# A fused causal convolution and spectral mixing kernel: other banks for the last mixings, another split of evictions in the second unit, and another route for the last bank

## The chip, the cores and the metric

The kernel runs on one core of a Trainium2 chip. The metric is the device time of one execution in microseconds. Three runs of the kernel before took 173.77, 173.94 and 174.34 us; the median, 173.94 us, is what the forecast is measured against. Beside these there is one profiled execution, of which the page and the trace tell.

## The reference

The input is x with 8 sequences of 3264 positions and 192 channels, in float32. Two stages follow each other.

The first is a causal convolution along the sequence. Each of 8 heads (24 channels each) has 7 taps, made by a softmax over its 7 weights:

```
w = softmax(weight, axis=-1)
out[b, s, h*24:(h+1)*24] = sum_k w[h, k] * x[b, s - 6 + k, h*24:(h+1)*24]
```

The second takes this output as its own x, and mixes it in frequency:

```
X  = rfft(x, axis=1)
Yr = einsum('bmd,mde->bme', Xr, w_r) - einsum('bmd,mde->bme', Xi, w_i)   # modes 0..63 only
Yi = einsum('bmd,mde->bme', Xr, w_i) + einsum('bmd,mde->bme', Xi, w_r)
y  = irfft(Y, n=3264, axis=1)                                            # all other modes are 0
u  = x + y
out = u + maximum(u @ w_ch, 0)
```

So each position gets u = x + y, and to it relu(u W) with a 192 by 192 matrix W.

## The kernel before, in words

Everything is in bf16 except the sums in PSUM and the output. The work is issued in the order in which it is written: the code runs under a manual schedule, so each engine's queue holds its instructions in program order, and semaphores for the data and for the buffers are added to it.

**Tiles.** The 8 sequences are taken as 4 pairs. A sequence is cut into blocks of 256 positions, 13 of them (the last has 192), and a block into its even and odd positions, which makes 26 tiles of 128 positions for a pair, 104 in all. `xall` holds x, and later the convolved x in its place. The last block's tiles use 96 partitions.

**Convolution (L288 to L345).** The pairs are cut into units, two for each pair; I number them 1 to 8. Units 1 and 2 belong to the first pair and have 5 and 8 blocks (`UNITS0`); the others have 7 and 6. For each unit the loop runs over the 8 heads, numbered 0 to 7, and for each head over the even and the odd positions. A head takes 16 small matmuls (L297), and its upper half lags two steps behind its lower half. For the first pair, a head's two results go to a tile of two PSUM banks, and there are four such tiles; one instruction then evicts both into `xall`, cast to bf16, on ScalarE (L334) or on VectorE (L336). Line 333 chooses between them. A tile goes back to the free list once it is evicted, and head h+4 takes the tile of head h. The tables of sine and cosine for the Fourier products are made in between (L192 to L210): VectorE works out the angles, ScalarE the sine. x comes in by DMA, issued by POOL (L153, L157), a unit at a time and in the order of the units; the weights of the mixing follow in the same queue (L276). Unit 1's convolution is followed by the first six Fourier products and three matmuls that write nothing that is used (L434).

**Fourier sums and mixing.** Products with the table `ftab` (L358) give the 64 modes, which are transposed (L375, L377) into `xt`. There are 16 mixings, numbered 0 to 15, of four modes each. A mixing (L510, L515) is 12 matmuls into the half of a bank; two mixings share one bank. ScalarE scales the result into `ymix` (L527), TensorE transposes it into two banks (L546 by way of L398), and VectorE (L552) and ScalarE (L554) copy the two into `yet`. Meanwhile the convolved x is transposed into `ct`.

**The products with W (L587 to L604).** For each pair of sequences, numbered 0 to 3, `zw_pair` multiplies `yet` by two halves of the weights: eight matmuls (L591, L592) into two banks, of which ScalarE evicts the first (L602) and VectorE the second (L604) into `zwl`. Pairs 1, 2 and 3 are done early, with the last eight modes still zero or incomplete in `yet`; `late_rows` works out those rows apart and sends them over the rows in `zwl` by 16 small DMAs. Pair 0 is done last, when `yet` is complete (L681 to L687).

**Banks of the mixing tail.** There are eight banks: `ze` (two) and `zm` (two) on the right side, and `sl` (four) on the left side, opened at L664. Before the change `place[0]` and `place[1]`, the banks of the first two row-tile pairs of the second stage, are all four of `sl`; `zw_pair(1)` and `zw_pair(3)` use `ze`, `zw_pair(2)` uses `zm`; mixing 14 goes to `zm[1]`, mixing 15 to `zm[0]`; and both transposes of a mixing go to `ze`.

**Second stage (L695 to L767).** It runs over 52 duos of an even and an odd tile, 104 items in all. For each item, matmuls (L711) compute u W into a bank, ScalarE applies the relu in place (L637), a matmul adds y to the same bank, and VectorE adds x and writes float32 to an output buffer (L624). The banks are handed out from a list of eight, `ring`, in turn. An item is worked on by halves of the array, so TensorE has several items open. The last two items take y in one full matmul each (`full`, L644). Once both items of a duo are added, SP issues one store (L632) of 384 KB, or 288 KB for the last duo of each pair of sequences. For the first and the last duo of all, each item is stored apart; the last duo's items are 144 KB each.

Of the kernel before, what the change touches and what calls it, by code (L numbers as in the profile page):

```python
# [9 lines left out]
ALU = mybir.AluOpType  # L10
# [10 lines left out]
def kernel(  # L21
# [9 lines left out]
    nc = tc.nc  # L31
    B, S, D = x.shape
# [8 lines left out]
    NT = 2 * NB  # L41
# [13 lines left out]
    def sb(name, shape, dtype):  # L55
        return pool.tile([P] + shape, dtype, tag=name, name=name)
# [6 lines left out]
    xall = sb("xall", [NSLOT, 2, D], BF16)  # L63
# [13 lines left out]
    ident = sb("ident", [P], BF16)  # L77
    perm = sb("perm", [P], BF16)
    apart = [sb(f"apart{i}", [P], BF16) for i in range(2)]
# [112 lines left out]
    def table(step, t0, t1):  # L192
# [15 lines left out]
        else:  # L208
# [5 lines left out]
                            in1=wmax.unsqueeze(2).to_broadcast([P, H, KK]), op=ALU.subtract)  # L214
# [11 lines left out]
    for h0 in (0, H // 2):  # L226
        hs = slice(h0, h0 + H // 2)
        for lag in range(KK):
            k = lag // 2
            nc.vector.copy_predicated(  # L230
                out=pk4[:, hs, lag % 2, :],
                mask=masks[:, PW * k:PW * (k + 1)].unsqueeze(1).to_broadcast([P, H // 2, PW]),
                data=ta3[:, hs, KK - 1 - lag:KK - lag].to_broadcast([P, H // 2, PW]))
        for g in range(4):
            c0 = 1 + 32 * (g % 2)
            dst, srcv = band[32 * g:32 * g + 32, hs, :, c0:c0 + PW], pk4[32 * g:32 * g + 32, hs, :, :]
# [34 lines left out]
    NG = MODES // 4  # L271

    def load_w(g):
        if g < NG:
            for half, src in ((0, moe_w_r), (1, moe_w_i)):
                nc.gpsimd.dma_start(out=wts[g][64 * half:64 * half + 64, :, :, :],  # L276
                                    in_=src[4 * g:4 * g + 4, :, :].rearrange("m (p j) e -> p m j e", j=3))

    def turn(names):
        nop = nc.tensor.nop()  # L280
        for name in names:
            tc.add_manual_dep(nop.ins, name, mybir.DependencyInfo(mybir.DependencyClass.Sync,
                                                                  mybir.DependencyReason.DATA),
                              reason="row tiles take turns on a bank")

    def conv_pieces(step, row):

        (q, b0, n, h, a), z, _ = step  # L288
        s0 = NB * q + b0 + 1
        r = slice(64 * row, 64 * row + 64)  # L290
        dsl = slice(GRP * h, GRP * h + GRP)
        for a1 in range(2):
            for col in (row, 1 - row):
                c0 = (0 if a < a1 else 1) + (64 if col != row else 0)
                s1 = s0 - 1 if (row, col) == (1, 0) else s0
                o = z[64 * col:64 * col + 64, 0:2 * GRP * n].rearrange("p (b i e) -> p b i e", b=n, i=2)
                yield nc.tensor.matmul(o, band[r, h, int(a != a1), c0:c0 + 64], xin5[r, s1:s1 + n, :, a1, dsl],  # L297
                                       start=(row == 0 and a1 == 0), stop=(row == 1 and a1 == 1),
                                       tile_position=(64 * row, 64 * col), skip_group_check=True).ins.name
# [4 lines left out]
    def conv_step(u):  # L304

        lower = upper = iter(())
        flow.append(None)
        if u is not None:
            if u[0]:
                z = free.pop(0)  # L310
            else:
                z = flow[-2][0][2] if u[4] else free.pop(0)
            flow[-1] = [(u, z[:, u[4] if u[0] == 0 else 0, :], z), []]
            lower = conv_pieces(flow[-1][0], 0)
        old = flow[-1 - CONVLAG] if len(flow) > CONVLAG else None
        if old is not None:
            upper = conv_pieces(old[0], 1)

        if u is not None:
            flow[-1][1].extend(lower)  # L320
        if old is not None:
            turn(old[1][2:])
            for _ in upper:
                pass
        if old is None or old[0][0][4] == 0:
            return
        (q, b0, n, h, _), _, tile1 = old[0]
        s0 = NT * q + 2 * b0
        dst = xall[:, s0:s0 + 2 * n, :, GRP * h:GRP * h + GRP].rearrange("p (b a) i e -> p a b i e", a=2)
        tile0 = flow[-2 - CONVLAG][0][2]  # L330
        if q == 0:
            srcv = tile0[:, :, 0:2 * GRP * n].rearrange("p a (b i e) -> p a b i e", b=n, i=2)
            if h not in (5, 7) if b0 == 0 else h % 2 == 0:
                nc.scalar.copy(out=dst, in_=srcv)  # L334
            else:
                nc.vector.tensor_copy(out=dst, in_=srcv)  # L336
            free.append(tile0)
        else:
            for a, z in enumerate((tile0, tile1)):
                srcv = z[:, 0, 0:2 * GRP * n].rearrange("p (b i e) -> p b i e", b=n, i=2)  # L340
                if a == 1:
                    nc.scalar.copy(out=dst[:, a], in_=srcv)  # L342
                else:
                    nc.vector.tensor_copy(out=dst[:, a], in_=srcv)  # L344
                free.append(z)  # L345

    def flush():
        for _ in range(CONVLAG):
            conv_step(None)
        flow.clear()  # L350
# [125 lines left out]
    ze, zm = [z[:, 0, :] for z in z4[0:2]], [z[:, 0, :] for z in z4[2:4]]  # L476
# [33 lines left out]
    def mix(g, bank):  # L510
        yp = bank[:, D * (g % 2):D * (g % 2) + D]
        for j in range(3):
            for p4 in range(4):
                m = 4 * g + p4
                nc.tensor.matmul(yp[32 * p4:32 * p4 + 2 * B, :], xt[:, j, :, m],  # L515
                                 wts[g][:, p4, j, :], start=(j == 0), stop=(j == 2),
                                 tile_position=(0, 32 * p4), skip_group_check=True)
        load_w(g + NW + NL)

    def mix_copy(d, bank, g0, n):  # L520

        g = 2 * d + g0
        srcv = bank[:, D * g0:D * (g0 + n)].rearrange("p (g d) -> p g d", g=n)
        if g == 0:
            nc.scalar.activation(out=ymix[:, 0, :], in_=srcv[:, 0, :], func=ACT.Copy, scale=ascale[:, 0:1])
            g, n, srcv = 1, n - 1, srcv[:, 1:n, :]
        nc.scalar.activation(out=ymix[:, g:g + n, :], in_=srcv, func=ACT.Copy, scale=2.0 / S)  # L527
# [66 lines left out]
    def zw_pair(q, bw, by):  # L594

        for t, bank in enumerate((bw, by)):
            for i in range(2):
                zw_mm(2 * q + i, bank[:, D * i:D * i + D], t)
        for t, bank in enumerate((bw, by)):
            dst, srcv = zwl[:, 2 * q - 2:2 * q, t, :], bank[:, 0:2 * D].rearrange("p (b d) -> p b d", b=2)  # L600
            if t == 0:
                nc.scalar.copy(out=dst, in_=srcv)  # L602
            else:
                nc.vector.tensor_copy(out=dst, in_=srcv)  # L604
# [9 lines left out]
    duos = [((q, 2 * b), (q, 2 * b + 1)) for q in range(NQ) for b in range(NB)]  # L614
    N = len(duos)
    place = {}

    def add(bank, n, a):

        o = outs[n % NO]  # L620
        q, t = duos[n][0]
        pn = PL if t == NT - 2 else P
        s = NT * q + t
        nc.vector.tensor_tensor(out=o[0:pn, :, a, :],  # L624
                                in0=bank[0:pn, 0:2 * D].rearrange("p (i d) -> p i d", i=2),
                                in1=xall[0:pn, s + a, :, :], op=ALU.add)
        apart = n in (0, N - 1)
        if apart or a == 1:
            a0, w = (a, 1) if apart else (0, 2)
            dst = bass.AP(tensor=out.tensor, offset=out.offset + (2 * q * S + P * t + a0) * D,  # L630
                          ap=[[2 * D, pn], [S * D, 2], [1, w * D]])
            nc.sync.dma_start(out=dst, in_=o[0:pn, :, a0:a0 + w, :].rearrange("p i a d -> p i (a d)"))  # L632
# [8 lines left out]
    def full(n, which, a):  # L641
        (q, t), _ = duos[n]
        r = zrhs(slice(0, P), which, q)
        nc.tensor.matmul(target(place[n][a], slice(0, 2 * D), r), ftab[:, t + a, :], r, start=False,  # L644
                         stop=(which == "y"), skip_group_check=True)
# [13 lines left out]
    d = ND - 2  # L659
# [2 lines left out]
    mix(2 * d + 1, zm[0])  # L662
    mix_copy(d, zm[0], 0, 2)
    sl = [z[:, 0, :] for z in open_psum("left", (1, 1, 1, 1))]  # L664
    place[0], place[1] = sl[0:2], sl[2:4]
    both(0, 0, "c", begin=True)
    mix_trans(d, 0, 2)
    both(0, 1, "c")
    zw_pair(1, ze[0], ze[1])
    zw_pair(2, zm[0], zm[1])  # L670
    d = ND - 1
    mix(NG - 2, zm[1])
    mix_copy(d, zm[1], 0, 1)
    zw_pair(3, ze[0], ze[1])
    mix_trans(d, 0, 1)
    mix(NG - 1, zm[0])
    mix_copy(d, zm[0], 1, 1)
    both(1, 0, "c", begin=True)
    mix_trans(d, 1, 1)
    both(1, 1, "c")  # L680
# [15 lines left out]
    LAG = 2  # L696
    items = [(n, a) for n in range(FIRST, N) for a in range(2)]
    K = len(items)
    ring = ze + zm[1:2] + sl + zm[0:1]
    taken = [0]  # L700

    def next_of_ring():
# [3 lines left out]
    bank = {}  # L706
# [23 lines left out]
    def lower_y(k):  # L730
        if 0 <= k < K - 2:
            product(k, 0, pieces(k, 0, "y")[0], False, False)
        elif K - 2 <= k < K:
            n, a = items[k]
            full(n, "y", a)
            add(bank[k], n, a)

# [62 lines left out]
```

## Time and profile before

| what | value |
|---|---|
| median of three runs | 173.94 us (173.77 to 174.34) |
| profiled execution | 173.73 us, of which the span is 171.9 us |
| TensorE matmuls | 161.4 us busy, 94% of the span |
| VectorE | 129.6 us busy, 75% |
| ScalarE | 113.1 us busy, 66% |
| the chain that ended last | TensorE 83%, VectorE 8%, ScalarE 3% |
| granted TensorE clock, mean | 0.997 |
| DMA | 39.10 MB read, 20.05 MB written |

The page's times are in microseconds from the first instruction. A line of the timeline or of the chain begins with its start and its length; then come the engine, the tile and the line of the kernel, and "x12" for a group of twelve instructions. In square brackets stands how long the engine was idle before it, and who released it. A matmul's row is longer than the distance to the next matmul, since they are pipelined. The span by stages, from the chain: convolution and Fourier sums up to some 72 us, mixing and transposes up to 105 us, second stage from 106 to 167 us, and the last stores.

### The profile page before, as it was taken

What the parts mean: (1) busy time and instruction counts of PE and PEld (TensorE: products, weight loads), DVE (VectorE), ACT (ScalarE), POOL (GpSimd) and SP (SyncE); (2) the same over time, 40 slices, a digit from 0 to 9 for tenths busy, and PEclk for the clock granted to TensorE, in tenths of its full rate; (3) what the DMA queues carried; (4) which work ended last, traced back from release to release, by engine and by line L of the source; (5) the groups of instructions that cost most, each with busy time, mean ns of one, the idle gap of its engine ahead of it and who ended that gap; (6) DMA issues with size and microseconds to landing.
All of it is one profiled execution on the core that took longest, in us unless ns stands there. A gap on an engine that the chain in (4) does not pass through costs nothing.

```text
span 171.9 us, 6922 instructions
## 1 busy us (share of the span) xinstructions
PE 161.4 (94%) x2896; PEld 134.8 (78%) x2896; DVE 129.6 (75%) x263; ACT 113.1 (66%) x225; POOL 51.4 (30%) x93
## 2 busy tenths in 40 slices
PE   6998899999998999979999979999999999999990
PEld 6994686877867777779999765699999999999960
DVE  4899974736737575567767734799999999999991
ACT  8485864545546366377777643688888888888870
POOL 7997522323322443444431000691000000000000
PEclk9999999999999999999999999999999999999998
DMA  3999999999999999999999940389989999899996
GB/s 28 201 203 203 207 201 203 204 203 202 205 202 205 208 205 206 207 206 206 209 204 207 209 79 4 105 305 328 372 322 338 348 330 343 317 366 341 338 349 219
DMA packets 37359, 40.14 MB, mean 233 GB/s; under 512 B 2480, under 2 KB 37328, under 8 KB 37328
## 3 DMA queue, kind: packets, MB, share of 16 engines
q0 software_dynamic: 22816, 19.62, 71.3%
q1 hardware_dynamic: 14512, 20.09, 31.9%
q8 instruction: 22, 0.36, 0.8%
q14 instruction: 9, 0.07, 0.1%
HBM read 39.10 MB, written 20.05 MB: 344 GB/s over the span
## 4 chain that ended last, share of the span: by engine, by line
PE 83%; DVE 8%; ACT 3%; issue 2%; POOL 1%; DVEq 0%; POOLq 0%; ACTq 0%
PE z L711 34%; PE z L297 19%; PE z L398 12%; PE z L358 10%; PE z L515 3%; DVE arena L230 2%; DVE xall L336 1%; POOL xall L153 1%; PE z L591 1%; PE z L644 1%; DVE shared L240 1%; PE z L375 1%; PE z L592 1%; DVE arena L604 1%; DVE arena L624 1%
## 5 line engine op out<-in xcount | busy, mean ns | idle before, releaser
L624 DVE TENSOR_TENSOR arena<-z,xall 128x384 f32<-128x384 f32 (+1 forms) x104 | 57.4, 557 | 2.9 <-PE z L711 0.8
L637 ACT ACTIVATE z<-z 128x384 f32<-128x384 f32 x102 | 48.5, 475 | 12.2 <-PE z L711 2.4
L711 PEld LDWEIGHTS <-ct 64*128 64x128 bf16 x600 | 42.4, 94 | 3.7 <-PE z L644 0.6
L711 PE MATMUL z<-arena,ftab 64*128 64x384 bf16 x308 | 44.9, 322 | 0.0
L297 PE MATMUL z<-xall,shared 64*64 64x336 bf16 (+3 forms) x1024 | 38.5, 294 | 1.2 <-DVE xall L336 0.7
L297 PEld LDWEIGHTS <-shared 64*64 64x64 bf16 x1024 | 33.2, 106 | 6.6 <-issue 4.4
L711 PE MATMUL z<-wsw,ct 64*128 64x192 bf16 x300 | 35.1, 243 | 0.0
L711 PEld LDWEIGHTS <-ftab 64*128 64x128 bf16 x396 | 29.7, 93 | 2.7 <-issue 0.5
L344 DVE CAST xall<-z 128x336 bf16<-128x336 f32 (+1 forms) x48 | 22.9, 483 | 11.5 <-PE z L297 9.0
L711 PE MATMUL z<-wm,ct 64*128 64x192 bf16 x200 | 29.9, 243 | 0.0
L342 ACT CAST xall<-z 128x336 bf16<-128x336 f32 (+1 forms) x48 | 19.9, 419 | 13.8 <-PE z L297 10.0
L711 PE MATMUL z<-w,ct 64*128 64x192 bf16 x100 | 24.3, 243 | 0.0
L395 DVE COPY ct<-z 128x1024 bf16<-128x1024 bf16 x27 | 17.4, 685 | 5.5 <-PE z L398 2.4
L398 PE MATMUL z<-ident,xall 128*128 128x128 bf16 x312 | 19.8, 219 | 0.0
L358 PE MATMUL z<-xall,ftab 128*128 128x384 bf16 (+1 forms) x104 | 18.3, 327 | 0.8 <-DVE xall L336 0.8
L398 PEld LDWEIGHTS <-xall 128*128 128x128 bf16 x312 | 17.8, 98 | 1.0 <-issue 0.2
L153 POOL DMA_DIRECT2D xall<-in_x_dram x16 | 15.0, 942 | 10.4 <-DMA xall<-in_x_dram 9.6
L358 PEld LDWEIGHTS <-ftab 128*128 128x128 bf16 (+1 forms) x104 | 9.6, 98 | 8.2 <-issue 1.5
L711 PE MATMUL z<-mixa,ftab 64*128 64x384 bf16 x88 | 13.6, 323 | 0.0
L393 ACT COPY ct<-z 128x1024 bf16<-128x1024 bf16 x12 | 12.2, 1013 | 2.1 <-PE z L398 1.9
L539 POOL DMA_DIRECT2D arena<-xs x16 | 7.9, 505 | 17.2 <-ACT xs L535 17.2
L184 PE MATMUL z<-xall 128*128 128x144 bf16 x85 | 8.1, 280 | 1.6 <-DVE xall L171 1.6
(110 smaller groups left out, 154.2 us busy)
## 6 DMA issues: line engine op xcount, KB each, us to landing
out_dram<-arena SPq DMA_DIRECT2D x47, 384.0 KB, 3.6
xall<-in_x_dram POOLq DMA_DIRECT2D x8, 672.0 KB, 16.9
xall<-in_x_dram POOLq DMA_DIRECT2D x8, 480.0 KB, 16.7
arena<-in_moe_w_r_dram POOLq DMA_DIRECT2D x10, 288.0 KB, 11.2
arena<-in_moe_w_i_dram POOLq DMA_DIRECT2D x10, 288.0 KB, 11.5
ct<-in_moe_w_r_dram POOLq DMA_DIRECT2D x6, 288.0 KB, 11.5
ct<-in_moe_w_i_dram POOLq DMA_DIRECT2D x6, 288.0 KB, 11.5
out_dram<-arena SPq DMA_DIRECT2D x3, 288.0 KB, 3.2
```

The costliest lines, as they stand in the source:

```text
L153: nc.gpsimd.dma_start(out=xin[:, s0:s0 + nf, 2 * D * i:2 * D * (i + 1)], in_=src)
L184: nc.tensor.matmul(free[3][:, 0, 0:144], zeros[:, 0:P], zeros[:, 0:144], start=True, stop=True, skip_group_check=True)
L297: yield nc.tensor.matmul(o, band[r, h, int(a != a1), c0:c0 + 64], xin5[r, s1:s1 + n, :, a1, dsl], start=(row == 0 and a1 == 0), stop=(row ...
L342: nc.scalar.copy(out=dst[:, a], in_=srcv)
L344: nc.vector.tensor_copy(out=dst[:, a], in_=srcv)
L358: nc.tensor.matmul(xp, ftab[0:k, t, :], xall[0:k, NT * q + t, :, :], start=(t == t0), stop=(t == t1 - 1), skip_group_check=True)
L393: nc.scalar.copy(out=out, in_=in_)
L395: nc.vector.tensor_copy(out=out, in_=in_)
L398: nc.tensor.matmul(o, in_, ident[:], start=True, stop=True, is_transpose=True)
L624: nc.vector.tensor_tensor(out=o[0:pn, :, a, :], in0=bank[0:pn, 0:2 * D].rearrange("p (i d) -> p i d", i=2), in1=xall[0:pn, s + a, :, :], o ...
L637: nc.scalar.activation(out=z, in_=z, func=ACT.Relu)
L711: mm = nc.tensor.matmul(target(bank[k], cols, r), l, r, start=first, stop=last, skip_group_check=True)
```

## The change

The change has three parts.

1. **Evictions in unit 2.** Line 333 gives heads 0, 1, 3 and 5 of unit 2 to ScalarE and heads 2, 4, 6 and 7 to VectorE. Before, ScalarE had the even and VectorE the odd heads. In unit 1 nothing changes (ScalarE has 0, 1, 2, 3, 4 and 6).
2. **Banks of the mixing tail.** Mixings 14 and 15 both go to `zm[1]`. The transposes of mixing 14 stay in `ze`, those of mixing 15 go to the two banks that `ze` is renamed to, `sl[2:4]`; `place[1]` gets the old `ze` in exchange. `zw_pair(2)` moves behind mixing 14 and uses `sl[2]` and `sl[3]`; `zw_pair(3)` moves behind the transposes of mixing 14 and uses `zm[0]` and `sl[2]`. The list `ring` is written so that the new banks take the old roles in it.
3. **The very last bank.** For the last item of all, TensorE multiplies the identity by x into the bank (384 columns), ahead of the product that adds y, and ScalarE copies the bank to the output buffer; VectorE adds nothing there. The last duo is stored by one DMA of 288 KB after both items, where there were two of 144 KB.

```diff
@@ conv_step
-            if h not in (5, 7) if b0 == 0 else h % 2 == 0:
+            if h in ((0, 1, 2, 3, 4, 6) if b0 == 0 else (0, 1, 3, 5)):
                 nc.scalar.copy(out=dst, in_=srcv)
             else:
                 nc.vector.tensor_copy(out=dst, in_=srcv)
@@ add
-        nc.vector.tensor_tensor(out=o[0:pn, :, a, :],
-                                in0=bank[0:pn, 0:2 * D].rearrange("p (i d) -> p i d", i=2),
-                                in1=xall[0:pn, s + a, :, :], op=ALU.add)
-        apart = n in (0, N - 1)
+        srcv = bank[0:pn, 0:2 * D].rearrange("p (i d) -> p i d", i=2)
+        if (n, a) == (N - 1, 1):
+
+            nc.scalar.copy(out=o[0:pn, :, a, :], in_=srcv)
+        else:
+            nc.vector.tensor_tensor(out=o[0:pn, :, a, :], in0=srcv, in1=xall[0:pn, s + a, :, :], op=ALU.add)
+        apart = n == 0
@@ mixing tail
-    place[0], place[1] = sl[0:2], sl[2:4]
+    place[0] = sl[0:2]
     both(0, 0, "c", begin=True)
     mix_trans(d, 0, 2)
     both(0, 1, "c")
     zw_pair(1, ze[0], ze[1])
-    zw_pair(2, zm[0], zm[1])
     d = ND - 1
     mix(NG - 2, zm[1])
     mix_copy(d, zm[1], 0, 1)
-    zw_pair(3, ze[0], ze[1])
+    zw_pair(2, sl[2], sl[3])
     mix_trans(d, 0, 1)
-    mix(NG - 1, zm[0])
-    mix_copy(d, zm[0], 1, 1)
+    zw_pair(3, zm[0], sl[2])
+    mix(NG - 1, zm[1])
+    mix_copy(d, zm[1], 1, 1)
+
+    place[1], ze = ze, sl[2:4]
     both(1, 0, "c", begin=True)
     mix_trans(d, 1, 1)
     both(1, 1, "c")
@@ second stage
-    ring = ze + zm[1:2] + sl + zm[0:1]
+    ring = ze + zm[1:2] + place[0] + place[1] + zm[0:1]
@@ lower_y, the last two items
             n, a = items[k]
+            if k == K - 1:
+                qt = NT * duos[n][0][0] + duos[n][0][1] + a
+                nc.tensor.matmul(bank[k][:, 0:2 * D], ident[:], xall[:, qt, :, :].rearrange("p i d -> p (i d)"),
+                                 start=False, stop=False, skip_group_check=True)
             full(n, "y", a)
             add(bank[k], n, a)
```

## The prediction on record

> **What bounds the kernel now.** I read the page first (share of each engine, the chain that ended last), then the chain of waits in order of time, and then the instructions of the three places that the change touches. TensorE works for 161.4 of 171.9 us and holds 83% of the chain. Time can only be won where the chain leaves TensorE, or at the very end. The change touches three such places: the convolution of unit 2 (around 21 us), the mixing tail (100 to 105 us) and the last two additions (167 us). The chain at the first, then at the second:
>
> ```profile
> 20.71 0.96 DVE xall L336
> 21.68 0.04 issue
> 21.72 5.74 PE z L297 x128
> ```
>
> ```profile
> 100.85 0.10 PE z L592
> 100.95 0.03 issue
> 100.97 0.57 DVE arena L604
> 101.54 0.04 issue
> 101.58 0.47 PE z L515 x12
> ...
> 102.88 0.02 issue
> 102.90 0.57 DVE arena L604
> 103.47 0.04 issue
> 103.51 0.22 PE z L398
> 103.73 0.42 PE z L515 x12
> ```
>
> The reader is to see VectorE evictions standing between TensorE pieces: one of head 1 (L336) in the first, two of L604 in the second. The other views I needed are when two transfers land, and the end.
>
> **Part 1, evictions of unit 2.** Unit 2 has four two-bank tiles for eight heads, so head h+4 starts only when head h has been evicted. Before, VectorE owns head 1, but its queue still holds the tables' steps until 20.79; the eviction runs 20.71 to 21.67 and TensorE idles from 21.07 to 21.72 (0.65 us) ahead of head 5. With the new split ScalarE takes head 1 right behind head 0 (19.21 to 20.01), 0.80 each by L334, so the tile is free at 20.8 and head 5 starts unhindered. VectorE's first eviction is now head 2, at the same 20.71 to 21.67, so head 6 starts at 21.72, where head 5 started before. Unit 2 is ahead by one head: 16 matmuls, which the ScalarE evictions of heads 0 and 2 (19.21 and 20.51, two heads apart) put at 0.65 us. The rest is evicted in time: ScalarE 0, 1, 3, 5 by 23.5, VectorE 2, 4, 6, 7 by 25.2; unit 3's first head is evicted at 25.85 in the trace, and only its fourth needs the last tile.
>
> But unit 3 needs its own x. It was issued as two transfers:
>
> ```profile
> L153 POOL DMA_DIRECT2D xall<-in_x_dram x2: 952/970/987, 6.3 to 7.2; - x2
> ...
> DMA to landing us min/median/max: 14.6/15.8/17.0
> ```
>
> The second was issued at 7.2 and took 17.0, so it landed at 24.2. Unit 3's first weight load is at 24.39, after 0.25 us idle with no engine named, its first matmul at 24.42. For unit 2 the last load landed at 5.2+12.3 = 17.5 and the first matmul came at 17.63; the same 0.1 us after landing puts unit 3 at 24.3 at the earliest. The x and weight stream runs at some 200 to 210 GB/s from 5 us to 99 us, so these landings don't move when TensorE gets faster. Of the 0.65 us, then, 0.10 is left and 0.55 turns into a wait for x. I count **0.10 us**, bounds 0 and 0.65. Everything from there to 100 us follows TensorE; the later x loads land over 2 us before use (the last at 42.1+13.4 = 55.5; its unit starts near 60.8).
>
> **Part 2, the mixing tail.** Durations are the rows' own: L602 0.48, L604 0.56, mixing 0.40 from first matmul to the next piece, a pair (8 matmuls of L591 and L592) 0.64, L552 0.19, L554 0.21, L527 0.33. Before: mixing 14 waits for the bank that pair 2 used (first matmul 101.58), pair 3 follows, its two transposes wait for L602 (103.05) and L604 (103.46), and mixing 15 starts at 103.66. After, on the clock of before:
> - Pair 1 as now, 99.40 to 100.11. Mixing 14 goes to a bank free since 93 us and starts at 100.11 (its weights landed at 88.2+11.2 = 99.4). L527 100.60 to 100.93.
> - Pair 2, into two banks of the new set, 100.51 to 101.24; L602 101.10 to 101.58, L604 101.43 to 101.99. The transposes run at 101.24 to 101.55, without waits, since pair 1's banks are free at 100.46 and 100.95.
> - A new wait: pair 3 now reads yet after mixing 14's copies wrote it. L552 stands behind pair 2's L604 on VectorE, 101.95 to 102.14. TensorE idles from 101.36 to 102.22; queued behind are pair 3, mixing 15 and all of the second stage.
> - Pair 3 at 102.22, mixing 15 at 102.94, L527 103.45 to 103.78, against 104.17 to 104.50 before. What follows is as before: transposes, copies, the unit-0 products.
>
> So TensorE's stalls of 0.81, 0.40 and 0.35 become one of 0.86: **0.72 us** won by L527's end. Bounds: nothing (all three stalls come back under new names), and 1.3, where mixing 15 would meet its weights, issued at 91.0:
>
> ```profile
> L276 POOL DMA_DIRECT2D arena<-in_moe_w_i_dram x1: 610/610/610, 91.0 to 91.0; - x1
> ...
> DMA to landing us min/median/max: 11.2/11.2/11.2
> ```
>
> They land at 102.2, and mixing 15 wants to start at 102.94 less part 1's 0.10: 0.5 us of cover is left after the 0.1 release. The second stage keeps its rhythm: the list of eight banks exchanges the roles of two pairs and nothing else, and TensorE goes on there without a gap to 166.3.
>
> **Part 3, the end.** Before, VectorE adds the last two items one after the other and two 144 KB stores follow:
>
> ```profile
> 166.57 0.47 ACT L637 ACTIVATE z<-z 128x384 f32<-128x384 f32 x1
> 166.67 0.75 PE L644 MATMUL z<-arena,ftab 128*128 128x384 bf16 x2
> 166.83 1.48 DVE L624 TENSOR_TENSOR arena<-z,xall 128x384 f32<-128x384 f32 x3
> 167.42 1.46 SPq L632 DMA_DIRECT2D out_dram<-arena  x3
> ```
>
> Three additions end at 168.32, the stores start at 167.42, 167.88 and 168.42, and the last lands at 168.42+2.5 = 170.92. After: the identity matmul goes at 167.10, behind ScalarE's clamp (ends 167.04), where the last product went, and adds one pitch of L644, 0.17, with its weight load under it. The product ends at 167.59 in place of 167.42. ScalarE, idle by then, copies in 0.48 (L361 and L637): 167.62 to 168.10. VectorE's last addition ends at 167.85, so the one store is issued at 168.13, 0.29 earlier, but it holds 288 KB. At the end the 384 KB store landed in 2.8 and the 144 KB one in 2.5; between them by size, 288 KB is 2.68, so it lands at 170.81: **0.10 us** won. Bounds: 0.41 lost, if it takes the 3.2 us of the three other 288 KB stores, which ran among others (171.33); 0.3 won, if it moves at the 395 GB/s of the larger store instead of the 250 to 350 GB/s seen after 169.2.
>
> The Trainium skill ("DMA: Bandwidth & Descriptors", Anatomy of one DMA) gives a transfer some 2.0 us of fixed cost plus its bytes at 436 GB/s. By that, an estimate, 144 KB takes 2.34 and 288 KB 2.68; the part would lose 0.05 instead of winning 0.10. The trace's 144 KB store took 2.5.
>
> **Sum.** 0.10 + 0.72 + 0.10 = 0.92 us. The profiled execution took 173.73 us, of which 171.9 is span; it becomes 172.8. The median of the runs, 173.94, lies 0.2 above it, so I forecast **173.0 us**.
>
> **Rivals.**
> - *Unit 3 isn't held by x.* Part 1 keeps its 0.65: 1.47 in all, 172.5 us. For: the trace names no DMA at 24.39. Against: 24.2 plus 0.1 leaves no room. Chance 0.12.
> - *The change doesn't do what it says in the tail*: the stalls at the transposes come back behind the new wait. 0.20 left, 173.7 us. For: the wait for yet is as long as the one removed (0.86 against 0.81). Against: no later step finds an occupied bank by my walk. Chance 0.10.
> - *The merged store lands late* (3.2 us): 0.82 less 0.41 is 0.41 won, 173.5 us. Chance 0.10.
> - *Slower, by TensorE's clock.* This trace shows it falling: the last matmul ends at 167.42, and the granted clock is 1.00 until 170.8, 0.71 in the next 0.2 us and 0.50 from 171.0. Were the new waits (0.55 at 23.7, 0.86 at 101.4) to bring that on, a stretch as long as the one that brought it down, 3.4 us, at half speed would cost 1.7: 174.7 us. It decides only where TensorE is idle for some 3.4 us. Against: the clock stays 1.00 through the idle second at 73.2 and the 0.65 at 21.1. Chance 0.04.
> - Forecast: 0.62; some other loss, 0.02.
>
> The Trainium skill ("TensorE: Matmul & The Clock Gate", What's actually happening) lets the clock halve after an idle window of about 3.4 us; the drop at 170.9 agrees, and by that rule too the new gaps are too short.
>
> A difference under 0.3% (0.52 us) can't be told from none. Faster takes the forecast and the first rival, with a remainder of the others, 0.75; within 0.3% the tail and the store, 0.20; slower 0.05. The range 172.4 to 173.6 covers forecast, first rival and late store, and leaves out 0.16.
>
> **What would show it.** Part 1: no idle TensorE at 21.1, but a gap of some 0.5 us before unit 3's first matmul, still near 24.3; if that comes near 23.8, part 1 was worth 0.65. Part 2: mixing 14 right behind pair 1, one gap of 0.8 to 0.9 before pair 3, released by L552, none at the transposes, and L527 of mixing 15 some 0.7 to 0.8 earlier. Part 3: one store in place of two, issued 0.3 earlier relative to the last clamp, landing after 2.6 to 2.8. A mixing matmul waiting for a weight transfer, or a second stage longer than the 56.6 us from 109.70 to 166.32, would prove me wrong.

## The result and the profile after

The changed kernel took 173.72 us (median of 22 runs, 173.07 to 174.15), the kernel before 174.15 us (22 runs, 173.77 to 174.89). The ratio is 0.9971, with a 95% interval of 0.996 to 0.9981: by the ratio 0.50 us faster (0.33 to 0.70; the two medians lie 0.43 apart), where 0.92 was forecast. The time lies just outside the range of 172.4 to 173.6. Of the 0.72 us between 173.0 and 173.72, 0.21 comes from the kernel before: the three runs that the forecast started from had a median of 173.94, and 22 runs have 174.15. The rest is gain that the change did not bring.

The profiled execution of the changed kernel took 173.94 us, with a span of 172.2, which is no faster than the one of before (173.73 and 171.9). Single executions of one kernel differ by more than the change is worth (173.07 to 174.15 for the changed one), so the two traces have to be compared place by place.

**Unit 3.** The chain of the changed kernel, in order of time:

```profile
7.24 17.17 DMA xall<-in_x_dram
24.41 0.14 issue
24.55 3.04 PE z L297 x72
```

The reader is to see a transfer where VectorE's eviction stood. TensorE's timeline has the other half (the first line is unit 2, the second unit 3):

```profile
17.63 6.54 PE L297 MATMUL z<-xall,shared 64*64 64x384 bf16 x128 [0.16 <-DMA xall<-in_x_dram]
24.55 3.04 PE L297 MATMUL z<-xall,shared 64*64 64x336 bf16 x72 [0.37 <-DMA xall<-in_x_dram]
```

Unit 2 now runs through without the 0.65 us in which TensorE stood idle before (the hole, from here on). Its last matmul ends at 24.17, and unit 3 waits 0.37 us for its x. It starts at 24.55, and before it started at 24.42: in this execution the transfer landed at 24.41, 0.2 later than in the one of before. So the first part lost 0.13 us here.

**The mixing tail.** The chain again:

```profile
101.52 0.10 PE z L592
101.61 0.02 issue
101.64 0.11 DVE arena L604
101.75 0.36 issue
102.11 0.19 DVE yet L552
102.31 0.05 issue
102.35 0.30 PE z L591
...
103.23 0.42 PE z L515 x9
103.66 0.02 issue
103.68 0.34 ACT shared L527
```

Of the two evictions that stood between TensorE's pieces, one wait is left, and it is the new one: L552 behind L604, 0.64 us of idle TensorE before pair 3. Mixing 15 runs at 103.16 in place of 103.66, and the first product of pair 0 at 104.64 in place of 105.13. That is 0.49 us, or 0.62 counted from unit 3's start. The second stage keeps its pace: its last product starts 0.33 earlier (166.77 in place of 167.10) although the identity matmul (0.16) now goes ahead of it.

**The end.** The timeline:

```profile
166.61 0.32 PE L742 MATMUL z<-xall,ident 128*128 128x384 bf16 x1
166.61 0.10 PEld L647 LDWEIGHTS <-ftab 128*128 128x128 bf16 x1 [0.32 <-issue]
166.77 0.32 PE L647 MATMUL z<-arena,ftab 128*128 128x384 bf16 x1
166.93 1.04 SPq L635 DMA_DIRECT2D out_dram<-arena  x2
167.13 0.47 ACT L627 COPY arena<-z 96x384 f32<-96x384 f32 x1 [0.57 <-PE z L647]
```

The last store is issued at 167.64 instead of 168.42: the 0.49 that came down, and 0.29 from the new route of the last bank. Yet it lands no earlier (a store lands when its last part has arrived). The stores of the last two microseconds, before and then after (the first line counts them and gives their starts, the second their time from issue to landing):

```profile
L632 SPq DMA_DIRECT2D out_dram<-arena x4: 372/410/450, 166.3 to 168.4; - x4
...
DMA to landing us min/median/max: 2.5/2.7/2.9
```

```profile
L635 SPq DMA_DIRECT2D out_dram<-arena x3: 335/372/372, 165.8 to 167.6; - x3
...
DMA to landing us min/median/max: 3.5/3.5/3.6
```

The last one lands at 167.64+3.5 = 171.1, against 168.42+2.5 = 170.9. And the merged store, the one of 288 KB, isn't slow by itself: the 384 KB stores ahead of it took as long. To see where that comes from, one goes back 9 us, to the stores issued from 157.2 to 158.3 before and from 156.7 to 159.0 after:

```profile
L632 SPq DMA_DIRECT2D out_dram<-arena x2: 372/372/372, 157.2 to 158.3; - x2
...
DMA to landing us min/median/max: 2.8/3.5/4.1
```

```profile
L635 SPq DMA_DIRECT2D out_dram<-arena x3: 372/372/373, 156.7 to 159.0; - x3
...
DMA to landing us min/median/max: 3.1/4.6/4.8
```

From one store to the next the landing jumps by 1.3 us (2.8 to 4.1) before, and by 1.7 (3.1 to 4.8) after. In both, one packet of the queue that the profile names "instruction" falls there, between 157 and 160. The DMA view, with the share of 16 engines' time over these 3 us as its last column, before and after:

```profile
q8 instruction: 1, 0.02, 2.7%
```

```profile
q8 instruction: 1, 0.02, 4.0%
```

2.7% of 16 engines' 3 us is 1.3 us of one engine, 4.0% is 1.9: about the two jumps. From there the landing time falls by some 0.15 us with every store, one each 1.14 us, until the kernel ends: to 2.5 before, to 3.5 after. That is the rate at which a late engine can catch up: at the 397 GB/s seen from 168.4 to 169.0, 384 KB take 1.0 us, an estimate, and 0.14 are left over. The DMA's last microsecond shows the same thing: in the changed kernel its share from 170.0 to 170.8 is 0.06 to 0.17, one to three engines of 16. In the kernel before, all engines are busy up to 170.2 and only the 0.2 us from 170.4 have a share of 0.11, so there the delay had all but gone by the end. So a theory for the end: one DMA engine that carried the instructions is behind with its part of every store, and the last landing is when it has caught up. Stores that are issued earlier wait there.

### The profile page after: what moved, and what is told of

Same layout as the page of the kernel before. It is cut to its first block, busy times and chain, and to the rows that moved or that the text cites. A ratio compares the mean times of both kernels' runs of the same rounds, so it can differ in the third digit from the quotient of the medians.

```text
span 172.2 us, 6925 instructions
## 1 busy us (share of the span) xinstructions
PE 160.6 (93%) x2897; PEld 133.6 (78%) x2897; DVE 128.5 (75%) x262; ACT 113.7 (66%) x226; POOL 51.4 (30%) x93
## 4 chain that ended last, share of the span: by engine, by line
PE 79%; DMA 10%; POOL 3%; ACT 2%; issue 1%; DVE 1%; POOLq 0%; ACTq 0%; DVEq 0%
PE z L716 34%; PE z L297 16%; PE z L398 12%; DMA xall<-in_x_dram 10%; PE z L358 10%; PE z L515 3%; POOL xall L153 3%; PE z L591 1%; PE z L647 1%; PE z L375 1%; PE z L592 1%; ACT ftab L393 1%; ACT z L479 1%; ACT shared L527 0%; PE z L582 0%
## 5 line engine op out<-in xcount | busy, mean ns | idle before, releaser
L629 DVE TENSOR_TENSOR arena<-z,xall 128x384 f32<-128x384 f32 (+1 forms) x103 | 56.4, 556 | 3.4 <-PE z L716 1.5
L297 PE MATMUL z<-xall,shared 64*64 64x336 bf16 (+3 forms) x1024 | 39.0, 294 | 2.1 <-ACT shared L238 1.1
L297 PEld LDWEIGHTS <-shared 64*64 64x64 bf16 x1024 | 33.2, 106 | 8.1 <-issue 4.3
L716 PE MATMUL z<-w,ct 64*128 64x192 bf16 x100 | 24.3, 243 | 0.0
L276 POOL DMA_DIRECT2D arena<-in_moe_w_r_dram x10 | 6.1, 615 | 9.9 <-ACT xall L342 4.7
```

Source lines behind the costliest of these rows:

```text
L629: nc.vector.tensor_tensor(out=o[0:pn, :, a, :], in0=srcv, in1=xall[0:pn, s + a, :, :], op=ALU.add)
L716: mm = nc.tensor.matmul(target(bank[k], cols, r), l, r, start=first, stop=last, skip_group_check=True)
```

## The experiments

Theory A, with which I went into them: only the mixing tail pays; unit 3 is held by its x; the end is set by the DMA engine that is behind. The rivals are named in each expectation. Times are medians, ratios are to runs of the kernel before on the same chip.

**One part alone.** Line 333 by itself:

```diff
-            if h not in (5, 7) if b0 == 0 else h % 2 == 0:
+            if h in ((0, 1, 2, 3, 4, 6) if b0 == 0 else (0, 1, 3, 5)):
```

> Part 1 alone (the other split of unit 2's evictions). Theory A, unit 3 is held by the landing of its x: no difference to before (within 0.2 us); the idle 0.65 us at 21.1 is gone and a gap of 0.4 to 0.6 us stands before unit 3's first matmul, which starts 0.1 us after its x landed, at 24.3 to 24.6. Rival B, the split pays 0.65 us and the change loses it somewhere behind: 0.5 to 0.7 us faster, unit 3 starting near 23.8.

Measured: ratio 1.0015 (0.9997 to 1.0032), 174.34 us against 174.22: no gain. The hole in unit 2 is gone and the wait for x is there, in this execution behind a landing at 25.10:

```profile
18.43 6.54 PE L297 MATMUL z<-xall,shared 64*64 64x384 bf16 x128 [1.04 <-DMA xall<-in_x_dram]
25.23 3.04 PE L297 MATMUL z<-xall,shared 64*64 64x336 bf16 x72 [0.26 <-DMA xall<-in_x_dram]
```

Both units start right behind a landing, 0.7 to 0.8 us later than in the other two traces; the start of 25.23 misses the 24.3 to 24.6 that I expected, but it is the landing plus 0.13. So a late x stream moves the whole run (this profiled execution took 175.48 us, the slowest of the twelve). Rival B falls.

The mixing tail by itself, with line 333, `add` and the last two items as before:

```diff
-    zw_pair(2, zm[0], zm[1])
...
+    zw_pair(2, sl[2], sl[3])
     mix_trans(d, 0, 1)
+    zw_pair(3, zm[0], sl[2])
+    mix(NG - 1, zm[1])
```

> Part 2 alone (other banks and order in the mixing tail). Theory A: the first product of pair 0 starts 0.6 us earlier relative to unit 3's start, and the run is 0.5 to 0.7 us faster than before, so this part makes all of the change's gain. Rival B, the tail's gain is lost again behind (second stage or last stores): under 0.3 us faster.

Measured: ratio 0.9969 (0.9951 to 0.9987), 0.54 us faster: as much as the whole change. Theory A holds by the times; the interval, 0.23 to 0.85 us, reaches just below the rival's 0.3. The sign in the profile came out at 0.2 us in place of 0.6, counted from unit 3's start: in this execution TensorE waited 0.86 us at 55.1, for something that the profile doesn't name, where it had waited 0.44 before. Counted from the transposes behind that wait (68.96, before 68.49), the first product of pair 0 comes 0.63 us earlier.

This kernel has the old split, and its trace shows how much of the hole is chance:

```profile
21.52 2.80 PE L297 MATMUL z<-xall,shared 64*64 64x384 bf16 x56 [0.41 <-DVE xall L336]
24.47 3.04 PE L297 MATMUL z<-xall,shared 64*64 64x336 bf16 x72 [0.15 <-DMA xall<-in_x_dram]
```

The hole is 0.41 us here, where the prediction took its 0.65 from one execution, and behind it unit 3 waits for its x even with the old split.

The end by itself, part 3 added to the kernel before:

> Part 3 alone (x by TensorE into the last bank, ScalarE evicts it, one store of 288 KB for the last duo). Theory A, the last landing is set by one DMA engine that is still behind since an instruction transfer near 158 us: the last eviction ends 0.2 to 0.3 us earlier, the last store lands no earlier, and the time is the same within 0.2 us. Rival C, the merged store itself is the loss: 0.3 to 0.5 us slower, landing over 3 us after its issue even where the stores before it land in under 2.9. The prediction on record said 0.1 us faster.

Measured: ratio 1.0004 (0.9979 to 1.0029). No gain and no loss that could be told; the interval reaches from 0.4 us faster to 0.5 slower, so a loss of 0.3 isn't excluded by the time alone. In the profile the merged store took 3.4 us and the one ahead of it 3.3, so it is no slower than its neighbours. The traces of the two kernels that keep the old end say the same: the two 144 KB stores took 3.4 and 3.2 us with line 333 alone, and 3.5 and 3.4 with the tail alone, where the one execution of the kernel before had 2.7 and 2.5. Over the last 0.8 us of these two the DMA share is 0.04 to 0.08, some one engine of 16. That speaks against rival C.

The whole change with two stores at the end:

```diff
-        apart = n == 0
+        apart = n in (0, N - 1)
```

> The whole change, but the last duo keeps its two stores of 144 KB (x by TensorE and ScalarE's eviction stay). Theory A (a DMA engine that is behind): the same as the change, 0.3 to 0.6 us faster than before, and the last landing follows the latency of the stores before it. Rival C (merging costs): 0.8 to 1.0 us faster than before, the last store landing 2.5 us after its issue.

Measured: ratio 0.9973 (0.9954 to 0.9991), as the change. The last store took 2.8 us, the two ahead of it 3.0 and 2.9, and the one at the jump, issued at 157.8, 4.3. Rival C, that merging costs, falls.

**Is unit 3 held by its x?** One size is changed so that its x is shorter, with the old split and with the new:

```diff
-    units = [(q, b0, n) for q in range(NQ) for b0, n in (UNITS if q else UNITS0)]
+    UNITS1 = ((0, 6), (6, 7))
+    units = [(q, b0, n) for q in range(NQ) for b0, n in (UNITS0, UNITS1, UNITS, UNITS)[q]]
```

> The kernel before, but the second pair of sequences is cut into units of 6 and 7 blocks in place of 7 and 6. Unit 3's x is 192 KB shorter and lands about 0.9 us earlier, near 23.3. Theory A (with the old split unit 2 itself is just as late as the x was): the gain is what was left between the two, 0 to 0.2 us. Rival B (x never held unit 3): no difference, and none with the new split either.

> The same sizes (6 and 7 blocks) with part 1 added. Theory A: now that the x lands before unit 2 is done, the split's 0.55 to 0.65 us is paid: unit 3's first matmul near 23.8 and the run 0.5 to 0.8 us faster than before. Rival B: the split is worth nothing for another reason, the run is within 0.2 us of before.

Measured: with the old split 0.9975 (0.9958 to 0.9991), 0.44 us faster, which is more than I expected; with the new one 0.9943 (0.9926 to 0.9961), 0.99 us faster. Unit 3's x now lands at 23.4 and 23.6. With the new split, units 2 and 3 run in one piece up to the next Fourier products (this kernel has one line more, so L297 is L298 here):

```profile
17.63 8.84 PE L298 MATMUL z<-xall,shared 64*64 64x384 bf16 x200 [0.43 <-DMA xall<-in_x_dram]
26.41 1.80 PE L359 MATMUL z<-xall,ftab 128*128 128x384 bf16 x10
```

So the split is worth 0.55 us (0.9975 to 0.9943) once x is there, and nothing before. By the two intervals that is some 0.1 to 1.0 us; in the two profiles the transposes behind the convolution start 0.50 us apart (68.02 and 67.52). The old split's own 0.44 isn't all explained. In that profile VectorE's tables were done 0.7 us earlier than before: they began 0.3 earlier, and a step that took 0.91 took 0.49, so head 1's eviction began at 20.00 in place of 20.71. That shortened the hole in unit 2 to 0.17. Why that step was shorter stays open. And where the hole is short by itself, as in the trace of the tail alone, the old split waits for x too, so a shorter x pays there; how often that is so, no run tells.

**Is the new wait for yet on the path?** Pair 3 goes ahead of the transposes, so that it reads nothing of theirs:

```diff
     zw_pair(2, sl[2], sl[3])
+    zw_pair(3, zm[0], ze[0])
+    swap, ze = ze, [ze[1], sl[2]]
     mix_trans(d, 0, 1)
-    zw_pair(3, zm[0], sl[2])
+    ze = swap
     mix(NG - 1, zm[1])
```

> The whole change, with pair 3 moved ahead of the transposes of mixing 14 (into zm[0] and ze[0]; those transposes go to ze[1] and sl[2]), so that pair 3 no longer reads what L552 has just written. If the wait for yet (TensorE idle 0.6 to 0.7 us before pair 3) is on the path: mixing 15 starts some 0.8 us earlier, at its weights' landing near 102.1 to 102.3, the products before unit 0's copies some 0.4 us earlier, and the run is 0.3 to 0.5 us faster than the change (0.8 to 1.0 faster than before). If the stalls come back at other banks: the same as the change, 0.5 us faster than before.

Measured: ratio 0.9934 (0.9912 to 0.9956), 1.15 us faster than before and 0.65 faster than the change (by the two intervals some 0.2 to 1.1). Mixing 15 starts at 102.41 in place of 103.16, pair 0 at 104.10 in place of 104.64. The wait was on the path.

**Does a DMA engine that is behind set the end?** Six stores are left out, so that it can catch up (this kernel doesn't write all of the output):

```diff
         apart = n == 0
+        if N - 8 <= n < N - 2:
+            return
```

> The whole change, but six duos near the end (the eighth to the third from the last) are not stored, so part of the output is not written. If a DMA engine that lags since the instruction transfer near 158 us sets the end: it catches up, the last store lands 2.2 to 2.6 us after its issue in place of 2.8 to 3.5, and the run is 0.6 to 1.1 us faster than the change (1.1 to 1.6 faster than before). If the last store's time is its own (fixed cost and its 288 KB): the same as the change, 0.5 us faster than before.

Measured: ratio 0.9929 (0.9912 to 0.9945), 0.73 us faster than the change (0.9971 to 0.9929). Up to the gap the stores behave as in the change, and then they land in a microsecond less; first the stores around 157, then the last two:

```profile
L637 SPq DMA_DIRECT2D out_dram<-arena x3: 373/373/373, 156.6 to 158.9; - x3
...
DMA to landing us min/median/max: 3.2/4.6/4.8
```

```profile
L637 SPq DMA_DIRECT2D out_dram<-arena x2: 334/353/372, 166.9 to 167.6; - x2
...
DMA to landing us min/median/max: 2.4/2.5/2.6
```

Here the 384 KB store, with nothing ahead of it, takes 2.4 us, and the merged store, 0.7 us behind it, 2.6; in the change, behind the late stores, both take 3.5. That a backlog sets the end is shown by this. That it is a single engine's rests on the share of about one engine in sixteen at the end, and that this engine is the one that carried the instructions is argued from the times and sizes of the two jumps; the trace doesn't tell the engines apart.

**Both repairs together**, the sizes (6 and 7 blocks) and pair 3 first, added to the change:

> The whole change with both repairs: units of 6 and 7 blocks for the second pair, and pair 3 ahead of the transposes of mixing 14. If the weight stream is a floor: mixing 15 would start near 101.9 by the rest, but its weights land at 102.0 to 102.3 whatever TensorE does, so it starts 0.1 us after that, and the run is only 0 to 0.2 us faster than with pair 3 first alone (1.1 to 1.4 faster than before). If the gains add up: 1.5 to 1.8 us faster than before, mixing 15 at 101.9.

Measured: 172.77 us, ratio 0.9909 (0.9889 to 0.993), 1.59 us faster than before and the fastest complete version here. The floor is there: mixing 15 now waits for its weights. The chain (L516 is L515 here):

```profile
91.02 11.16 DMA arena<-in_moe_w_i_dram
102.18 0.04 issue
102.23 0.48 PE z L516 x11
```

It starts only 0.18 earlier than with pair 3 first alone, as the floor demands. But the run gained more than I had put for a floor, and its interval (1.22 to 1.93 us) can't tell the two expectations apart, nor this run for certain from the one with pair 3 first alone. In the profile pair 0 starts at 103.70 in place of 104.10, since VectorE gets done with pair 3 while mixing 15 waits; with pair 3 first alone, the products at L582 waited 0.21 us for that eviction.

## Why the prediction failed, point by point

- **Part 1 (0.10 us; the wait for x).** The mechanism was right: the hole moved from 21.1 to unit 3's first matmul, and the time was lost to a landing that TensorE can't move. The rival that would have kept 0.65 us fell. The size was off by 0.2 in the profile (0.13 lost), because the landing itself differs from run to run: 24.2, 24.41 and 25.10 in the traces shown, and between these in the five others with the same sizes. The hole differs as well (0.17 to 0.65 us in the four traces with the old split). A tenth of a microsecond between two times that both move can't be forecast from one execution. Alone the part gave nothing.
- **Part 2 (0.72 us).** It gave 0.62 in the profile and 0.54 alone (0.23 to 0.85). The order of waits was as forecast, and the stall before pair 3 is released by L552. Mis-sized was TensorE's change from a pair to a mixing: the prediction took 0.08 us, the distance between two matmuls of a pair, and it is 0.17 to 0.18 (100.15 to 100.33, 102.99 to 103.16), which is lost once, ahead of mixing 15. (Ahead of mixing 14 it is lost too, but the wait behind it shrinks by as much.)
- **Part 3 (0.10 us).** The issue came 0.29 us earlier, just as forecast. The step that failed is "between them by size, 288 KB is 2.68": a store's time to landing at the end of this kernel isn't so much a matter of its size as of how far the DMA is behind, and that had ended at 2.5 to 2.9 in the one execution that the prediction had. In the changed kernel's it was 3.5, so the part lost where 0.10 was forecast; in the medians it is worth nothing (1.0004 alone, and 0.9973 against 0.9971 with two stores). The rival of the late store came near the time (3.2 us, and 173.5 for the run) by luck, since its reason was wrong: it blamed the merged store.
- **The rule on transfers.** By the Trainium skill ("DMA: Bandwidth & Descriptors", Anatomy of one DMA), 2.0 us and the bytes at 436 GB/s, the merged store takes 2.68 us, an estimate. The page gives this as a fit for transfers that GpSimd issues, and here SP issues the stores. Free of the backlog the merged store took 2.6, behind it 3.5: the term that decides here is one that the rule doesn't hold.
- **The sum.** 0.92 became 0.50 (0.33 to 0.70): some 0.55 to 0.6 from part 2, nothing from parts 1 and 3. Of the shortfall, parts 1 and 3 make 0.10 each and part 2 some 0.2, but with intervals of 0.3 us on each part the runs can't rank them. Measured against the later median of the kernel before, the same forecast would have been 173.2 us. Two of three terms rested on the meeting of TensorE's time with a transfer's, and the prediction had allowed for their spread in the bounds but put the forecast and the narrow range on single values.
- **The clock.** TensorE's granted clock stayed at 1.00 through the new gaps; the slower rival didn't come up. After the last matmul it fell to 0.50 at 168.2, 1.1 us after it, where it had taken 3.4 before; in the nine traces of the experiments it took some 1.5 to 4.2. So the rival's "some 3.4 us" was not a fixed delay, and one trace could not give it.

## What to carry to other kernels

When an engine is let run ahead, look for the next time that it can't move: a stream that runs at one rate all along (203 to 207 GB/s here) lands when it lands, and the gain up to there is gone (unit 3's x at 24.4, mixing 15's weights at 102.2). For unit 3 it could be had by shortening what is ahead in the stream, which here was one changed size.

A move that takes away a wait for a bank can put in a wait for data; here the data were not even needed, and the pair only had to go ahead of the copies that wrote them (0.65 us).

A store's time to landing at the end of a kernel like this says how far the DMA is behind more than how large the store is (at this end 144 KB took 2.5 to 3.5 us, 384 KB 2.4 to 3.6). Read the landing of the stores before it, back to the last jump.

## What was not expected of the hardware

From 114 us on, every jump in the landing of the stores of the second stage goes with a transfer of the instruction queue: in the kernel before these fall in the stretches from 114, 122, 130, 136, 144, 152 and 158 us (2 us each), and the stores issued around 114.6, 122.6, 129.7, 136.6, 143.4, 151.4 and 158.3 are the ones that take 0.2 to 2.3 us longer than those ahead of them. (Ahead of 114 the landing climbs from 2.0 to 3.4 us without one, while the first stores and the small transfers of `late_rows` run.) A transfer of 0.02 MB thus costs up to 1.9 us of one engine, reckoned from its share, and the stores carry it along for over 9 us.

The landings of unit 3's x (24.2 to 25.10 in eight traces) came with the same issue time of 7.2 us. Executions of one kernel spread over a microsecond, and the traces differ by tenths up to a whole one in at least three places: the x stream, the unnamed wait of TensorE at 55 us (0.14 to 0.86), and the end.
